# A decode kernel with gradients: products that stream 8 or 16 columns in place of 64, larger score units, and another order for the w1 rows

## The chip, the cores and the metric

The kernel runs on one core of one Trainium2 chip. The metric is the time of one execution on the device, in microseconds. The kernel before was timed three times: 2059.57, 2062.02 and 2064.87 us, median 2062.02. One execution was also recorded by the hardware profiler.

TensorE (PE in the profile) multiplies: it loads a 128 x 128 block as weights (PEld) and then streams the columns of the other operand past it. VectorE (DVE) and ScalarE (ACT) copy, reduce and evaluate functions. GpSimd (POOL) copies here and issues the output transfers. SyncE (SP) issues the input transfers. A transfer is a DMA.

## The reference

Two layers, attention and a squared-ReLU MLP, are run twice over with the same weights on one token of width 1024, and then everything is differentiated.

```
x = A_x
x = x + attention(layernorm(x), K, V, wq, wo)     # L1
x = x + mlp(layernorm(x), w1, b1, w2, b2)         # L2
x = x + attention(layernorm(x), K, V, wq, wo)     # L3, the same K and V
x = x + mlp(layernorm(x), w1, b1, w2, b2)         # L4
outputs: x, and the gradients of x, K, V, wq, wo, w1, b1, w2, b2 for a given grad_out
```

The attention has 32 query heads of width 128 in 4 groups of 8; each group shares one K and one V of 65,536 keys. K and V are 64 MiB each, in bfloat16. A score is q.k / sqrt(128), then a softmax over all 65,536 keys, then the sum of V with these weights. Both attention layers read the same K and V, so the gradients of K and V are sums over the two.

## The kernel before, in words

**Chunks, items, groups.** A chunk is 128 keys: one 128 x 128 block of K and one of V. A group has 512 chunks (`C`), an item is 8 chunks, so a group has 64 items (`IPG`). K and V come in slabs of 32 chunks (1 MB) into slots of SBUF. A `Ring` hands out the least recently used slot; SP issues the loads in program order and stands still until the slot of the next load is free. The slots are `area[0]` to `area[13]`; 6 to 13 are halves of four pairs.

**Four passes over K and V.** The forward of L1, the forward of L3, pass 3 (the backward of L3, `attn_bwd3`) and pass 4 (the backward of L1, which also forms the gradients of K and V for both layers, `attn_bwd4`). `pipeline` (line 455) writes the order out: at step i each stage of a pass works on item i minus its lag, and then the background tasks due at this step (`bg`, filled by `at`) are emitted. Every engine follows that order.

**Forward (`attn_fwd`, line 517).** `kT` transposes the 8 blocks of an item on TensorE, and ACT or DVE copies them out of PSUM (`evac` picks the less loaded of the two, lines 153 and 156). `kS`, two steps later, multiplies each transposed block with the group's queries. The 8 queries of a group are 8 columns, but `L["qpad"]` holds them 8 times over, 64 columns, and all 64 are streamed (line 557). The product of chunk c is written to the columns of slot c and of the seven slots behind it; the next chunk overwrites those, and only the first 8 columns of each remain. For that a bank of 64 slots holds a unit of 56 chunks (`UB`). After a unit ACT copies its scores to SBUF and DVE takes their maximum (lines 562 and 563). After the last unit of a group `stats` takes the exponentials, 8 on ACT (line 586). `v8`, 12 steps after the group's last scores, multiplies V with the weights: 8 heads by 8 neighbouring chunks, 64 columns, of which 8 are used (line 600).

**Pass 3.** V is transposed (line 741) and multiplied with the gradient of the output (`vS`, line 761): 64 columns, where `dOpad` has zeros in all but the first 8, so the rest adds nothing. A first product per unit writes a bias to the whole bank (line 757). DVE multiplies with the weights (line 767), and `k8` multiplies K with the result (line 783), again 64 columns with 8 used.

**Pass 4** does this for both layers at once: 16 columns used of 64 in `vS` (line 855, `DOB`), units of 24 chunks (`UB4`), 8 of 64 in `k8` (line 893). Per unit DVE forms X (lines 864 and 865, with copies by GpSimd in 866 and 867), TensorE transposes X (line 872), and two products of 512 columns for every four chunks form the gradients of K and V (line 899), which ACT and DVE copy to a staging slot and GpSimd sends out (906, 907). X has three buffers (`XS`), its transposes three (`XT`). The weight gradients (`outer2`, line 949) run as background tasks.

**The w1 rows of L4 (`fetch_w1`, line 997).** L4 needs w1 as eight blocks of rows of 917 KB. They are fetched at the end of the forward of L3, in background steps counted from `ik`, the step after the last score product. Scores of a group are kept in a pair of slots: the third group's in slots 12 and 13, the last group's in 10 and 11, where the exponentials read them.

Of the kernel before, what the change touches and what calls it, by code (L numbers as in the profile page):

```python
# [8 lines left out]
BF = mybir.dt.bfloat16  # L9
# [9 lines left out]
def kernel(  # L19
# [42 lines left out]
    SLOTS = 512 // R  # L62
    UB = SLOTS - 8
# [3 lines left out]
    SL4 = 512 // R2  # L67
    UB4 = SL4 - 8
# [409 lines left out]
    def set_q(L, pq, at_, gs):  # L478
        for i, g in enumerate(gs):
            nc.vector.tensor_copy(out=L["qT"][:, g * R:(g + 1) * R], in_=pq[:, (at_ + i) * R:(at_ + i + 1) * R])  # L480
            nc.vector.tensor_copy(out=L["qpad"][:, g, :, :], in_=L["qT"][:, g * R:(g + 1) * R].unsqueeze(1).to_broadcast([P, 8, R]))
# [26 lines left out]
    def new_layer(x, lname):  # L508
# [4 lines left out]
        L["qpad"] = vec.tile([P, G, 8, R], BF, name=lname + "_qpad")  # L513
# [3 lines left out]
    def attn_fwd(L, order, eT, s_areas, more=None, keep=(), have=()):  # L517
# [26 lines left out]
        def kS(idx):  # L544
            g, c8 = kit[idx]
            if c8 == 0:
                state["S"] = s_areas[order.index(g) % 2].bitcast(F32).rearrange("p (r c) -> p r c", c=C)
                state["pm"] = tmp.tile([P, R, (C + UB - 1) // UB], F32, name="pm_all")
            S_sb, pm_all = state["S"], state["pm"]
            kt = state.pop(("kt", idx))  # L550
            for i in range(8):
                c = c8 + i
                slot = c % UB
                if slot == 0:
                    state["ps_s"] = ps_sc([P, SLOTS, R])
                ps_s = state["ps_s"]
                nc.tensor.matmul(ps_s[:, slot:slot + 8, :].rearrange("p a b -> p (a b)"), lhsT=kt[:, i, :],  # L557
                                 rhs=L["qpad"][:, g, :, :].rearrange("p a b -> p (a b)"), start=True, stop=True)
                if slot == UB - 1 or c == C - 1:
# [165 lines left out]
    def attn_bwd3(L, og, order, eT, dqT, bg):  # L725
# [6 lines left out]
        dOpad = vec.tile([P, G, 8, R], BF, name=lname + "_dOpad")  # L732
        nc.vector.memset(dOpad[:], 0.0)
# [12 lines left out]
        def vS(idx):  # L746
            g, c8 = kit[idx]
            if c8 == 0:
                nc.vector.tensor_copy(out=dOpad[:, g, 0, :], in_=og.dOT[:, g * R:(g + 1) * R])
                nc.vector.tensor_copy(out=ndt[:, :, :], in_=og.nd2[:, g * R:(g + 1) * R].unsqueeze(1).to_broadcast([64, SLOTS, R]))  # L750
            vt = state.pop(("vt", idx))
            for i in range(8):
                c = c8 + i
                slot = c % UB
                if slot == 0:
                    state["ps_dp"] = ps_sc([P, SLOTS, R])
# [3 lines left out]
                last = (slot == UB - 1 or c == C - 1)  # L760
                nc.tensor.matmul(ps_dp[:, slot:slot + 8, :].rearrange("p a b -> p (a b)"), lhsT=vt[:, i, :],  # L761
                                 rhs=dOpad[:, g, :, :].rearrange("p a b -> p (a b)"), start=False, stop=last)
                if last:
                    un = slot + 1
                    c0 = c - slot
                    dsT = dst.next().rearrange("p (s r) -> p s r", r=R)
                    nc.vector.tensor_tensor(out=dsT[:, 0:un + 8, :], in0=ps_dp[:, 0:un + 8, :],
                                            in1=eT[g][:, :, c0:c0 + un + 8].rearrange("p h c -> p c h"), op=ALU.mult)
                    add_load(dve=0.07 + (un + 8) * R * 0.0019)
                    state[(g, c0 // UB)] = dsT  # L770

        def k8(idx):
# [4 lines left out]
            if c8 == 0:  # L777
                state["ps_dq"] = ps_acc([P, 8, R])
            ps_dq = state["ps_dq"]
            for i in range(8):  # L780
                c = c8 + i
                sl = c - u * UB
                nc.tensor.matmul(ps_dq[:, :, :].rearrange("p a b -> p (a b)"), lhsT=kb8[:, i, :],
                                 rhs=dsT[:, sl:sl + 8, :].rearrange("p a b -> p (a b)"), start=(c == 0), stop=(c == C - 1))
            if c8 + 8 == C:
                nc.vector.scalar_tensor_tensor(out=dqT[:, g * R:(g + 1) * R], in0=ps_dq[:, 0, :], scalar=SCALE,
# [4 lines left out]
    def attn_bwd4(La, Lb, oga, ogb, order, eTa, eTb, dqT, bg, group_done, streams):  # L791
# [4 lines left out]
        XT = Turn([blocks(small, i) for i in range(3, 6)])  # L796
        XW = (UB4 + 1) * R4
        XS = Turn([part(small[:, 6144:], i, XW) for i in range(2)] + [part(area[5], 0, XW)])
        GGS = Turn([part(area[5][:, XW:], i, 512) for i in range(2)])
        NSL = UB4 + 4  # L800
        ndt4 = small[0:64, 6144 + 2 * XW:6144 + 2 * XW + NSL * R2].rearrange("p (s r) -> p s r", r=R2)
        ST = Turn([pair[6], pair[8], pair[10]])
        DOB = vec.tile([P, G, 4, R2], BF, name="DOB")
# [391 lines left out]
```

## Time and profile before

| | |
|---|---|
| profiled execution | 2060.59 us |
| its span, first to last instruction | 2058.8 us |
| median of the three timed runs | 2062.02 us |
| mean granted TensorE clock | 0.898 |
| TensorE busy | 1636.8 us (80%) |
| VectorE, ScalarE, GpSimd busy | 1139.3, 1037.8, 200.4 us |
| moved by DMA | 809.62 MB, mean 393 GB/s |

The granted clock is the share of the TensorE clock that a throttle let through: 1.0 or 0.5 at any moment, and the mean over a window or slice in the tables. "DMA share" is the mean busy share of the core's 16 DMA engines. In a list of instructions "x24" counts them; "<-" behind an idle time names what ended it.

### The profile page before, as it was taken

The page shows a single profiled execution, that of the slowest core. Times are in us where ns is not written, and L with a number is a line of the kernel's source. Part 1 is how long each engine was busy: PE and PEld are TensorE (multiplying, and loading weights), DVE is VectorE, ACT ScalarE, POOL GpSimd, SP SyncE. Part 2 cuts the span into 40 slices and gives each one's busy share as a digit, 9 for nine tenths or more (in the row PEclk, how much of TensorE's full clock was granted, in tenths as well). Part 3 has the DMA queues.
Part 4 walks back from the last instruction along what each step waited for, and adds up shares of the span by engine and source line. Part 5 has one row for each costly group of instructions (what it writes and reads, how often), then busy time and mean ns, then how long its engine had stood idle before and what let it go on. Part 6 is the DMA issues. An engine that isn't in the chain of part 4 may idle for free.

```text
span 2058.8 us, 66212 instructions
## 1 busy us (share of the span) xinstructions
PE 1636.8 (80%) x29852; PEld 1332.2 (65%) x29852; DVE 1139.3 (55%) x1887; ACT 1037.8 (50%) x1325; POOL 200.4 (10%) x386
## 2 busy tenths in 40 slices
PE   7888886588898847788888765779888978988876
PEld 7878776578787737677777664456555545655544
DVE  4544431255444303744444557668777767768856
ACT  4543432125433302444444537768666756767855
POOL 0000000000000000000000001213222222222221
PEclk9999997579999956899999987989999999998988
DMA  9999999999999998999999997899999999998996
GB/s 381 416 417 414 412 417 407 392 358 416 414 415 414 383 392 312 345 417 414 414 417 387 401 387 309 342 347 422 401 423 417 413 424 384 424 422 339 424 423 275
DMA packets 140079, 809.62 MB, mean 393 GB/s; under 512 B 13844, under 2 KB 13844, under 8 KB 58644
## 3 DMA queue, kind: packets, MB, share of 16 engines
q1 hardware_dynamic: 112884, 639.70, 76.7%
q0 software_dynamic: 26912, 165.69, 19.7%
q8 instruction: 233, 3.82, 0.7%
q14 instruction: 50, 0.41, 0.0%
HBM read 639.64 MB, written 165.69 MB: 391 GB/s over the span
## 4 chain that ended last, share of the span: by engine, by line
DMA 41%; PE 31%; ACT 12%; DVE 10%; issue 5%; SPq 0%; POOL 0%; ACTq 0%; DVEq 0%; POOLq 0%
DMA out_dram<-pair 11%; DMA slot<-in_A_k_cache_dram 7%; DMA slot<-in_A_v_cache_dram 7%; DMA pair<-in_A_v_cache_dram 5%; PE ps_tr L539 5%; PE ps_sc L557 4%; ACT small L153 4%; DMA pair<-in_A_k_cache_dram 3%; DMA pair<-in_A_wo_dram 3%; PE ps_gg L899 3%; PE ps_acc L600 2%; PE ps_tr L836 2%; ACT pair L153 2%; PE ps_tr L741 2%; DVE pair L156 2%
## 5 line engine op out<-in xcount | busy, mean ns | idle before, releaser
L156 DVE COPY small<-ps_tr 128x1024 bf16<-128x1024 bf16 (+1 forms) x650 | 438.8, 686 | 387.5 <-PE ps_tr L539 207.5
L153 ACT COPY small<-ps_tr 128x1024 bf16<-128x1024 bf16 (+1 forms) x414 | 394.5, 967 | 431.3 <-PE ps_tr L539 248.8
L153 ACT CAST pair<-ps_gg 128x1024 bf16<-128x1024 f32 x289 | 289.9, 1015 | 144.5 <-PE ps_gg L899 100.5
L156 DVE CAST pair<-ps_gg 128x1024 bf16<-128x1024 f32 x223 | 272.3, 1221 | 105.2 <-PE ps_gg L899 79.1
L899 PE MATMUL ps_gg<-slot,small 64*128 64x512 bf16 x1024 | 202.8, 400 | 69.8 <-ACT pair L153 30.1
L557 PE MATMUL ps_sc<-L_qpad,small 128*128 128x64 bf16 x3712 | 178.4, 196 | 26.3 <-ACT small L153 14.0
L539 PE MATMUL ps_tr<-ident_b,slot 128*128 128x128 bf16 x2304 | 163.1, 224 | 15.5 <-DMA slot<-in_A_k_cache_dram 11.5
L557 PEld LDWEIGHTS <-small 128*128 128x128 bf16 x3712 | 141.8, 99 | 45.1 <-ACT small L153 25.2
L600 PE MATMUL ps_acc<-eT,slot 128*128 128x64 bf16 x2720 | 131.1, 210 | 44.9 <-DMA slot<-in_A_v_cache_dram 42.3
L539 PEld LDWEIGHTS <-slot 128*128 128x128 bf16 x2304 | 137.2, 100 | 17.5 <-DMA slot<-in_A_k_cache_dram 14.1
L600 PEld LDWEIGHTS <-slot 128*128 128x128 bf16 x2720 | 114.9, 107 | 49.4 <-DMA slot<-in_A_v_cache_dram 46.6
L899 PEld LDWEIGHTS <-small 64*128 64x128 bf16 x1024 | 58.4, 94 | 112.5 <-issue 82.1
L836 PE MATMUL ps_tr<-ident_b,slot 128*128 128x128 bf16 x1440 | 128.3, 229 | 0.4 <-DVE small L156 0.2
L539 PE MATMUL ps_tr<-ident_b,pair 128*128 128x128 bf16 x1600 | 114.3, 224 | 14.4 <-DMA pair<-in_A_k_cache_dram 13.7
L836 PEld LDWEIGHTS <-slot 128*128 128x128 bf16 x1440 | 90.8, 102 | 50.6 <-issue 46.5
L761 PE MATMUL ps_sc<-B_dOpad,small 128*128 128x64 bf16 x2048 | 101.0, 196 | 25.4 <-ACT small L153 17.6
L855 PE MATMUL ps_sc<-DOB,small 128*128 128x64 bf16 x2048 | 118.1, 198 | 0.0
L855 PEld LDWEIGHTS <-small 128*128 128x128 bf16 x2048 | 92.4, 101 | 35.9 <-issue 27.3
L539 PEld LDWEIGHTS <-pair 128*128 128x128 bf16 x1600 | 95.4, 100 | 17.4 <-DMA pair<-in_A_k_cache_dram 15.4
L761 PEld LDWEIGHTS <-small 128*128 128x128 bf16 x2048 | 78.6, 100 | 42.9 <-ACT small L153 27.2
L949 PE MATMUL ps_gg<-pair 128*128 128x512 bf16 x240 | 80.0, 412 | 27.9 <-ACT pair L153 16.1
L382 ACT ACTIVATE slot<-slot 128x1024 bf16<-128x1024 bf16 (+1 forms) x75 | 84.1, 1123 | 19.1 <-DVE slot L381 18.4
(275 smaller groups left out, 2437.6 us busy)
## 6 DMA issues: line engine op xcount, KB each, us to landing
slot<-in_A_v_cache_dram SPq DMA_DIRECT2D x164, 1024.0 KB, 17.7
slot<-in_A_k_cache_dram SPq DMA_DIRECT2D x159, 1024.0 KB, 11.8
out_dram<-pair POOLq DMA_DIRECT2D x128, 1024.0 KB, 17.8
pair<-in_A_k_cache_dram SPq DMA_DIRECT2D x82, 1024.0 KB, 19.9
pair<-in_A_v_cache_dram SPq DMA_DIRECT2D x80, 1024.0 KB, 20.0
out_dram<-eT POOLq DMA_DIRECT2D x41, 512.0 KB, 18.8
slot<-in_A_wq_dram SPq DMA_DIRECT2D x25, 768.0 KB, 11.1
slot<-in_A_wo_dram SPq DMA_DIRECT2D x16, 1024.0 KB, 12.8
```

The costliest lines, as they stand in the source:

```text
L153: nc.scalar.copy(out=out, in_=in_)
L156: nc.vector.tensor_copy(out=out, in_=in_)
L382: nc.scalar.activation(out=view, in_=view, func=ACTF.Copy, accum_out=ycol)
L539: nc.tensor.transpose(pt[:, i, :], kb8[:, i, :], ident_b[:, :])
L557: nc.tensor.matmul(ps_s[:, slot:slot + 8, :].rearrange("p a b -> p (a b)"), lhsT=kt[:, i, :], rhs=L["qpad"][:, g, :, :].rearrange("p a b - ...
L600: nc.tensor.matmul(ps_o[:, :, :].rearrange("p a b -> p (a b)"), lhsT=vb8[:, i, :], rhs=eT[g][:, :, c:c + 8], start=(c == 0), stop=(c == C ...
L741: nc.tensor.transpose(pt[:, i, :], vb8[:, i, :], ident_b[:, :])
L761: nc.tensor.matmul(ps_dp[:, slot:slot + 8, :].rearrange("p a b -> p (a b)"), lhsT=vt[:, i, :], rhs=dOpad[:, g, :, :].rearrange("p a b -> p ...
L836: nc.tensor.transpose(pt[:, i, :], vb8[:, i, :], ident_b[:, :])
L855: nc.tensor.matmul(ps_dp[:, slot:slot + 4, :].rearrange("p a b -> p (a b)"), lhsT=vt[:, i, :], rhs=DOB[:, g, :, :].rearrange("p a b -> p ( ...
L899: nc.tensor.matmul(pg[:, t2 * 512:(t2 + 1) * 512], lhsT=xt[64 * t2:64 * t2 + 64, blk0 + half, :], rhs=GG[64 * t2:64 * t2 + 64, :, :, :].re ...
L949: nc.tensor.matmul(pg[:, q0:q0 + qq], lhsT=av[:, kb + kk, :], rhs=b_rows[:, n0 + m0 + q0:n0 + m0 + q0 + qq], start=True, stop=True)
```

## The change

The products of `kS`, `vS` and `k8` stream only the columns that are used: 8, and 16 in pass 4's `vS`. The padded operands (`qpad`, `dOpad`, the wide `DOB`) become plain ones (`qb`, `dOb`, `DOB`). The value product of the forward (`v8`) keeps its 64 columns. As no slots behind a unit are needed any more, a unit fills its bank: 64 chunks in place of 56 in the forward and pass 3, and 32 in place of 24 in pass 4, so a group has 8 units (10 before) and 16 (22 before). The lag of `k8` follows from the unit: one step more in pass 3 and pass 4. In pass 4 X and its transposes have two buffers in place of three, all in `small`. The rows of w1 go to slots 12, 13, 10, 11, 9, 8, 7, 6 at steps 1, 3, 16, 20, 24, 28, 33, 38 behind `ik`; before, to 10, 11, 12, 13, 9, 8, 7, 6 at 1, 3, 5, 7, 12, 18, 24, 30. Slot 5 leaves the ring at step 44 in place of 36.

```diff
-    SLOTS = 512 // R
-    UB = SLOTS - 8
+    UB = 512 // R
...
-    SL4 = 512 // R2
-    UB4 = SL4 - 8
+    UB4 = 512 // R2
...
-            nc.vector.tensor_copy(out=L["qpad"][:, g, :, :], in_=L["qT"][:, g * R:(g + 1) * R].unsqueeze(1).to_broadcast([P, 8, R]))
+            nc.vector.tensor_copy(out=L["qb"][:, g * R:(g + 1) * R], in_=L["qT"][:, g * R:(g + 1) * R])
...
-                nc.tensor.matmul(ps_s[:, slot:slot + 8, :].rearrange("p a b -> p (a b)"), lhsT=kt[:, i, :],
-                                 rhs=L["qpad"][:, g, :, :].rearrange("p a b -> p (a b)"), start=True, stop=True)
-                if slot == UB - 1 or c == C - 1:
+                nc.tensor.matmul(ps_s[:, slot, :], lhsT=kt[:, i, :], rhs=L["qb"][:, g * R:(g + 1) * R], start=True, stop=True)
+                if slot == UB - 1:
...
-                nc.tensor.matmul(ps_dp[:, slot:slot + 8, :].rearrange("p a b -> p (a b)"), lhsT=vt[:, i, :],
-                                 rhs=dOpad[:, g, :, :].rearrange("p a b -> p (a b)"), start=False, stop=last)
+                nc.tensor.matmul(ps_dp[:, slot, :], lhsT=vt[:, i, :], rhs=dOb[:, g * R:(g + 1) * R], start=False, stop=last)
...
-                nc.tensor.matmul(ps_dq[:, :, :].rearrange("p a b -> p (a b)"), lhsT=kb8[:, i, :],
-                                 rhs=dsT[:, sl:sl + 8, :].rearrange("p a b -> p (a b)"), start=(c == 0), stop=(c == C - 1))
+                nc.tensor.matmul(ps_dq[:, :], lhsT=kb8[:, i, :], rhs=dsT[:, c - u * UB, :], start=(c == 0), stop=(c == C - 1))
...
-        XT = Turn([blocks(small, i) for i in range(3, 6)])
-        XW = (UB4 + 1) * R4
-        XS = Turn([part(small[:, 6144:], i, XW) for i in range(2)] + [part(area[5], 0, XW)])
+        XT = Turn([blocks(small, i) for i in (3, 4)])
+        XS = Turn([part(small, i, 1024) for i in (5, 6)])
...
-                nc.tensor.matmul(ps_dp[:, slot:slot + 4, :].rearrange("p a b -> p (a b)"), lhsT=vt[:, i, :],
-                                 rhs=DOB[:, g, :, :].rearrange("p a b -> p (a b)"), start=False, stop=last)
+                nc.tensor.matmul(ps_dp[:, slot, :], lhsT=vt[:, i, :], rhs=DOB[:, g, :], start=False, stop=last)
...
-                nc.tensor.matmul(ps_dq[:, :, :].rearrange("p a b -> p (a b)"), lhsT=kb8[:, i, :],
-                                 rhs=X[:, sl:sl + 2, :].rearrange("p a b -> p (a b)"), start=(c == 0), stop=(c == C - 1))
+                nc.tensor.matmul(ps_dq[:, :], lhsT=kb8[:, i, :], rhs=X[:, c - u * UB4, 0:R], start=(c == 0), stop=(c == C - 1))
...
-        for k, i in enumerate((10, 11, 12, 13)):
-            at(bg, ik + 1 + 2 * k, lambda i=i: one(area[i]))
         at(bg, ik + 2, lambda: ring.remove(*area[6:10]))
-        for k, i in enumerate((9, 8, 7, 6)):
-            at(bg, ik + 12 + 6 * k, lambda i=i: one(area[i]))
-        at(bg, ik + 36, lambda: ring.remove(area[5]))
+        for k, i in ((1, 12), (3, 13), (16, 10), (20, 11), (24, 9), (28, 8), (33, 7), (38, 6)):
+            at(bg, ik + k, lambda i=i: one(area[i]))
+        at(bg, ik + 44, lambda: ring.remove(area[5]))
...
-    LAG4 = 6
+    LAG4 = 7
```

## The prediction

> **What bounds the kernel now.** I read the page first, then a table of stages, then the clock in its own steps.
>
> ```profile
> PEclk9999997579999956899999987989999999998988
> DMA  9999999999999998999999997899999999998996
> ...
> HBM read 639.64 MB, written 165.69 MB: 391 GB/s over the span
> ...
> DMA 41%; PE 31%; ACT 12%; DVE 10%; issue 5%; SPq 0%; POOL 0%; ACTq 0%; DVEq 0%; POOLq 0%
> ```
>
> The DMA engines are full in nearly every slice, and the granted TensorE clock is high in nearly every slice. The windows of the stages say it sharper (after each engine's busy time: granted clock, DMA share, GB/s):
>
> ```profile
> 27.00:330.00 303.00, 253.02 (x5732) 236.75 (x5730) 130.58 (x229) 129.79 (x192) 0.00 (x0) 0.96 1.01 413
> 460.00:710.00 250.00, 215.24 (x4931) 203.07 (x4927) 113.21 (x196) 106.93 (x156) 0.00 (x0) 0.97 1.01 415
> 850.00:1215.00 365.00, 302.00 (x6393) 269.88 (x6390) 184.74 (x297) 158.53 (x204) 0.00 (x0) 0.95 1.00 405
> 1280.00:1390.00 110.00, 81.41 (x1080) 53.98 (x1079) 76.01 (x116) 80.37 (x107) 22.26 (x42) 0.89 0.86 327
> 1390.00:1850.00 460.00, 399.39 (x5151) 258.03 (x5152) 346.55 (x484) 314.81 (x337) 124.47 (x237) 0.96 1.01 414
> 1850.00:2050.00 200.00, 160.55 (x1904) 101.69 (x1903) 152.29 (x212) 141.41 (x177) 45.71 (x86) 0.88 0.92 379
> ```
>
> Rows one and two are the forward passes, three is pass 3, four to six are pass 4. Memory traffic sets the pace except in row four and parts of row six. So fewer streamed columns buy nothing directly; what they can do is move the clock. The clock changes only at edges 3.41 us apart. Cut at those edges, a stretch with 64-column products alone (counts behind the first two busy times: matmuls and their weight loads):
>
> ```profile
> 351.42:354.83 3.41, 2.65 (x47) 2.49 (x48) 0.00 (x0) 0.00 (x0) 0.00 (x0) 0.50 1.01 420
> 354.83:358.25 3.42, 2.82 (x54) 2.66 (x51) 0.00 (x0) 0.00 (x0) 0.00 (x0) 0.50 1.02 414
> 358.25:361.66 3.41, 1.54 (x40) 1.28 (x38) 0.00 (x0) 0.00 (x0) 0.00 (x0) 1.00 1.02 423
> 361.66:365.07 3.41, 2.74 (x52) 2.58 (x51) 0.00 (x0) 0.00 (x0) 0.00 (x0) 0.50 1.01 401
> 365.07:368.49 3.42, 1.86 (x49) 1.59 (x46) 0.00 (x0) 0.00 (x0) 0.00 (x0) 1.00 0.94 367
> ```
>
> A step with 51 to 54 products is followed by a full-clock step, one with 47 or fewer by a half-clock step. So a step must stream about 49 x 64, some 3,100 columns, or the next one runs at half speed. That is my reading of these rows; one later step with 53 was followed by half, so the edge is soft.
>
> **Which columns the clock sees after the change.** A chunk is 128 keys: 64 KB of K and V, 158 ns at 415 GB/s, 21.6 chunks in a step. Columns per chunk, before and after: forward 128 (transpose) + 64 (score) + 64 (value product, untouched) = 256, then 200; pass 3 128+64+64 = 256, then 144; pass 4 128+64+32+64 and two 512-column products per four chunks that run side by side (two in 0.39 us, as long as one; counted once, 128) = 416, then 312, plus 60 of the weight gradients (240 products of 512 over 2,048 chunks). Pass 4 takes (2,050-1,280)/2,048 = 376 ns a chunk, 9.1 chunks a step. So a step streams in the forward 4,320 columns (5,530 before), in pass 3 3,110 at best and 2,760 at its mean of 365/2,048 = 178 ns (4,900 to 5,530 before), in pass 4 3,380 (4,320 before). The forward stays clear of 3,100, pass 3 falls onto or under it, pass 4 comes close.
>
> **Prices.** At full clock a transpose takes 56 ns (24 in 1.34 us), a 64-column product 29 (24 loads in 0.76 us), a 1-column one 25 (64 in 1.58 us). At half clock: 107 (24 in 2.56 us), 53 (54 in 2.82 us), and
>
> ```profile
> 1225.79 6.12 PE ps_bg L1074 x224
> ```
>
> 27 ns for one column. No row has 8 or 16 columns; they lie between the 1-column and the 64-column rows, 25 to 29 ns and 27 to 53. 128 and 64 columns at half clock are in proportion (107, 53), which gives 7 ns for 8, so the 27 ns is a floor; I take 25 and 27. If the load were not hidden, 27+7 = 34.
>
> **Part 1, w1 rows.** SP stands in line with a row meant for slot 10, which the last group's exponentials still read:
>
> ```profile
> 693.68 2.82 SPq L250 DMA_DIRECT2D pair<-in_A_v_cache_dram  x2
> 698.69 0.33 SPq L250 DMA_DIRECT2D slot<-in_A_v_cache_dram  x1
> 701.19 23.88 SPq L1000 DMA_DIRECT2D pair<-in_B_w_dram  x4
> ```
>
> Queued behind it are V slabs. The DMA share in the four 5 us windows from 710 is 0.77, 0.51, 0.54, 0.94: 6.2 us idle. Afterwards rows go first to slots 12 and 13, long free, and SP passes on to three V slabs (2 x 0.92 + 3 x 1.05 = 5.0 MB, 12 us) before it meets slot 10. That spans 711 to 723 of a wait that ends at 724. The value stage that follows is fed by DMA to 794, so the gain stays. I take -5.5; bounds -6.2 and 0 (the V slabs' own slots free too late). A loss is excluded: the last row's issue moves 8 steps and still lies 38 steps before that stage's end.
>
> **Part 2, score units of 64.** Units fall from 10 to 8 a group, but the group's last one grows from 64 elements (ACT 0.22, DVE 0.22 us) to 512 (0.53 and 0.62 for 448, so 0.60 and 0.70): exponentials start 0.86 us later. Three of four groups hide it behind the 12-step lag of the value product; the last groups of both passes don't. Half-clock steps in the forward cost TensorE 107+27+53 = 187 ns a chunk against 158 supplied, 0.6 us a step, and ten slots of 1 MB hide that (without them, some 23 such steps, +14). I take +1; bounds 0 and +14.
>
> **Part 3, pass 3.** TensorE needs 56+25+25+3 (the broadcast product) = 109 ns a chunk at full clock, 107+27+27+7 = 168 at half; supply is 158 to 178. At half clock and never idle a step streams 3,413/168 x 144 = 2,930 columns: mostly it stays at half, and the order of transposes and products within a step lifts some over the edge. The cover is thin: in the last group, with the w2 transposes (224 x 107 = 24 us), half-clock TensorE needs 512 x 168 + 24 = 110 us, about the 114 that the DMA needs, and the ring has five slots. Bounds: 0 (full-clock steps catch up), and +32 (34 ns each, so 182 ns a chunk: 2,048 x 182 + 24 = 397 against 365). I take +7, near the lower end, where the 1-column row puts it. The lag one step longer (K loads behind V) adds at most one step of 1.3 us and is in it.
>
> **Part 4, pass 4.** In the order transpose, product with V, transpose of X, broadcast, product with K, wide pair, TensorE needs 56+29+15+8+29+54 = 191 ns a chunk before and 56+25+14+7+25+54 = 181 after at full clock, 364 and 308 at half (107+53+28+16+53+107; 107+27+27+13+27+107), with the weight gradients 50 more: 358, under the 376 supplied. From 1,390 to 1,850 the DMA hides it; if staging slots come later for it, +3. Where the DMA isn't full (1,280 to 1,390, 1,860 to 1,880, 2,020 to 2,050: 160 us, 55 steps of eight chunks) the clock lies on the path. A clock of 0.89 is 22% half-clock steps: 8 x (0.78 x 191 + 0.22 x 364) = 1.83 us a step; with 55% after, 8 x (0.45 x 181 + 0.55 x 308) = 2.01. 55 x 0.18 = +10 if TensorE were the whole path there; the chain gives it about a third: +4. Units fall from 88 to 64 with DVE products of 256 elements for 200 (0.49 us; at 1.8 ns an element more 0.60): 88 x 0.98 - 64 x 1.20 = 9 us of DVE, a fifth of it in those stretches: -2. Two X buffers in place of three wait for nothing new: a unit's last reader runs three steps before the next writer. Sum +5; bounds -10 and +20.
>
> The Trainium skill speaks against this reading. "TensorE: Matmul & The Clock Gate", Part 4: transposes don't count as busy for the clock. By that rule pass 3 would show the gate 16 columns a chunk and stay at half throughout, my second rival. The trace disagrees: the first two of these steps hold 28 transposes each and otherwise single columns, and the step after each has the full clock.
>
> ```profile
> 1238.89:1242.30 3.41, 2.15 (x28) 1.59 (x28) 1.00 1.03 425
> 1242.30:1245.71 3.41, 2.15 (x28) 1.60 (x28) 1.00 1.01 420
> 1245.71:1249.13 3.42, 0.38 (x4) 0.23 (x4) 1.00 1.00 406
> ```
>
> **The sum.** -5.5 + 1 + 7 + 5 = +7.5 on the profiled execution of 2060.6 (span 2058.8, 1.8 around it): 2068.1. The median of the runs, 2062.0, is 1.4 higher: 2069.5, said as 2070.
>
> **Rivals.** Clock stuck: pass 3 stays at half and TensorE sets its pace. For it: 2,930 columns are under the edge. Against: it must need more than the supply. With 34 ns products +32 there, +10 in pass 4 (the whole path, above), -5.5: 2062 + 36.5 = 2098, or 2088 with pass 3 alone. Cover holds: slots and DMA hide every half-clock step and only part 1 is left: 2062 - 5.5 = 2056.5; for it, full DMA in nine tenths of the stages' time. Faster: half-clock steps themselves get cheaper (364 to 308). If their share stays at 25% where the DMA isn't full, a step there takes 8 x (0.75 x 181 + 0.25 x 308) = 1.70 for 1.83, 55 steps give -7, with part 1 2049; it decides below a share of 38%. Against: pass 4 falls to 3,380 columns a step. The w1 order does nothing, if SP then waits as long at slot 10 later, and the rest cancels: 2062.
>
> **How the numbers follow.** About 0.3% (6.2 us) is what a measurement of this kernel can tell from no change. Forecast (2063 to 2080) 0.42, of it 0.32 slower and 0.10 within; clock stuck 0.18, slower; cover holds 0.24, 0.14 faster and 0.10 within; faster 0.14; nothing 0.02, within. Together faster 0.28, within 0.22, slower 0.50. The range 2050 to 2096 leaves out the far ends of the stuck clock and of the faster case, some 0.17. The forecast's own range is 2063 to 2080.
>
> **What would show it.** Granted clock in pass 3 from 0.95 to about 0.6 to 0.75, with DMA share still 0.97 or more there (more idle DMA: stuck); forward clock 0.88 or more; pass 4 about 0.8. No DMA gap at 710 to 725. L783 at 27 ns in half-clock steps. A clock that stays at 0.9 in pass 3 makes my reading of the gate wrong; more than 385 us for pass 3 makes the 27 ns or the cover wrong.

## The result and the profile after

The changed kernel takes 2092.59 us (median of four runs, 2090.20 to 2096.58), the kernel before 2061.08 (2059.57 to 2064.87): a ratio of 1.0152, 95% interval 1.0129 to 1.0175. It is slower by some 31 us, where 8 were forecast; 2092.6 lies in the range of 2050 to 2096, near its far end, and outside the forecast's own 2063 to 2080. The profiled execution took 2090.20 us with a span of 2088.4, the mean granted clock is 0.809 (0.898 before).

From the page of the changed kernel, the clock and the DMA by slices, the traffic, and the chain by engine:

```profile
PEclk9999996569998855777767766876898889988896
DMA  9999999999999997999996998899999999999996
...
HBM read 639.64 MB, written 165.69 MB: 386 GB/s over the span
...
DMA 37%; PE 36%; DVE 12%; ACT 11%; issue 4%; POOL 0%; SPq 0%; DVEq 0%; ACTq 0%; POOLq 0%
```

The bytes are the same and move 1% slower on average. TensorE's share of the chain rose from 31% to 36%, DMA's fell from 41% to 37%. From the 17th slice on, at 835 us, the clock is lower than before in most slices. The same windows as before, of the changed kernel (behind the busy times: granted clock, DMA share, GB/s):

```profile
27.00:330.00 303.00, 253.10 (x5741) 235.25 (x5739) 128.67 (x221) 130.01 (x185) 0.00 (x0) 0.94 1.01 415
460.00:710.00 250.00, 217.58 (x4932) 204.27 (x4930) 110.37 (x191) 106.40 (x148) 0.00 (x0) 0.94 1.02 417
850.00:1215.00 365.00, 307.09 (x5909) 285.88 (x5907) 166.43 (x266) 147.96 (x188) 0.00 (x0) 0.74 0.95 377
1280.00:1390.00 110.00, 87.23 (x1134) 58.31 (x1135) 78.20 (x128) 74.75 (x94) 20.99 (x34) 0.74 0.81 308
1390.00:1850.00 460.00, 393.35 (x5085) 249.85 (x5082) 333.82 (x451) 306.76 (x329) 116.06 (x201) 0.87 1.00 407
1850.00:2050.00 200.00, 159.94 (x1984) 99.74 (x1985) 152.72 (x192) 143.56 (x173) 45.49 (x80) 0.83 0.98 403
```

Row three stands out: the clock of pass 3 fell from 0.95 to 0.74, and its traffic from 405 to 377 GB/s. The loss can be placed by SP's own list. SP issues the seventh slab of pass 3 at 827.7 us (833.6 before), so the changed kernel comes there 6 us early. The seventh slab of pass 4 is issued at 1273.4 (1251.3 before), 22 us late. Pass 3 lost 28 us. Inside it the lead of the loads shrinks slowly: 5 us at the 32nd load behind that one, 1.5 behind at the 64th, 6 to 8 behind at 1060. Up to 1060 the traffic is still that of the kernel before (409 GB/s from 850 to 1060 in both). Most of the loss in traffic shows at 1060 to 1130, 275 GB/s against 395. Windows of the changed kernel there, the second one a part of the first:

```profile
1060.00:1130.00 70.00, 62.57 (x1234) 58.94 (x1231) 25.49 (x37) 25.47 (x26) 0.00 (x0) 0.75 0.74 275
1105.00:1120.00 15.00, 13.63 (x290) 12.98 (x288) 4.97 (x7) 5.88 (x6) 0.00 (x0) 0.78 0.03 11
```

For 15 us almost nothing is loaded, while TensorE is busy for 13.6 of them. SP's list of the changed kernel has the reason (start, duration, line, transfer):

```profile
1099.75 0.64 SPq L248 DMA_DIRECT2D slot<-in_A_k_cache_dram  x1
1119.62 0.33 SPq L248 DMA_DIRECT2D slot<-in_A_v_cache_dram  x1
```

SP stands from 1100.4 to 1119.6 in front of a slot that still holds an earlier slab; in pass 3 only TensorE's transposes and products read the slabs. At this place of the program the ring shrinks from 13 slots to 5. The waits of SP from 850 to 1240 us that TensorE ended, by line (total us, times, longest; L737 is the transpose, L776 the product with K):

```profile
SPq L248 <- PE ps_tr L737: 136.3, 50, 5.4
SPq L248 <- PE ps_acc L776: 64.6, 32, 19.1
```

That is 201 us behind TensorE, and 58 behind the loads of slabs; in the kernel before it was 79 and 161. The loads of pass 3 used to wait for the DMA and now wait for TensorE.

**Why TensorE is late.** Cut at the clock's edges, six steps of the changed kernel in a row, all instructions (matmuls and weight loads counted behind the first two busy times):

```profile
1060.28:1063.69 3.41, 3.41 (x81) 3.41 (x80) 0.69 (x1) 2.02 (x2) 0.00 (x0) 0.50 1.03 413
1063.69:1067.10 3.41, 3.41 (x46) 3.41 (x43) 1.32 (x2) 1.01 (x1) 0.00 (x0) 0.50 1.00 360
1067.10:1070.52 3.42, 2.22 (x63) 1.83 (x62) 1.80 (x3) 0.00 (x0) 0.00 (x0) 1.00 0.96 347
1070.52:1073.93 3.41, 3.41 (x40) 3.41 (x41) 0.69 (x1) 1.75 (x2) 0.00 (x0) 0.50 0.94 368
1073.93:1077.34 3.41, 3.41 (x95) 3.30 (x93) 1.14 (x2) 1.50 (x3) 0.00 (x0) 1.00 0.87 312
1077.34:1080.76 3.42, 2.38 (x65) 1.94 (x62) 1.88 (x3) 0.76 (x1) 0.00 (x0) 1.00 0.91 299
```

The same steps, the transposes alone (line 737 of the changed kernel; PE, PEld, clock, DMA share, GB/s):

```profile
1060.28:1063.69 3.41, 1.93 (x17) 1.43 (x16) 0.50 1.03 413
1063.69:1067.10 3.41, 3.34 (x31) 3.12 (x32) 0.50 1.00 360
1067.10:1070.52 3.42, 0.37 (x6) 0.20 (x5) 1.00 0.96 347
1070.52:1073.93 3.41, 3.36 (x32) 3.09 (x32) 0.50 0.94 368
1073.93:1077.34 3.41, 1.89 (x31) 1.55 (x29) 1.00 0.87 312
1077.34:1080.76 3.42, 0.42 (x8) 0.25 (x5) 1.00 0.91 299
```

A step with 31 or 32 transposes (some 4,000 columns) is followed by full clock; a step with 6 transposes and otherwise products of 8 columns is followed by half. The first of these steps shows that being busy isn't enough: it is busy for all its 3.41 us with 81 products, but 17 transposes make at most some 2,700 columns, and the next step is at half clock. So the steps mostly alternate, and in the unlucky way: full clock falls to the products, which gain nothing from it (25 ns against 27), and half clock falls to the transposes, which cost twice as much. In the 57 steps from 862 to 1057 us, 31 are half-clock steps. Counted by their start, 626 of the 1,032 transposes, 61%, lie in them, but 37% of the products with V and 23% of the products with K. In the same 57 steps the edge can be bracketed, with the bias product as 512 columns: each step that streamed fewer than 3,104 columns was followed by half clock, each one with more than 3,456 by full clock, and between them both occur.

The second half of the answer is in the full-clock steps with few transposes: TensorE is idle in them for some 30% of the time. At 1069 us, lines of the changed kernel's timeline (the unit's DVE product, then the bias product that opens the next unit):

```profile
1069.04 1.04 DVE L761 TENSOR_TENSOR small<-ps_sc,eT 128x512 bf16<-128x512 f32 x1 [0.85 <-PE ps_sc L757]
...
1070.13 0.37 PE L753 MATMUL ps_sc<-small,sel 64*128 64x512 bf16 x1 [0.73 <-DVE small L761]
```

What TensorE waits for from 860 to 1060 (total us, times, longest):

```profile
PE ps_sc L753 <- DVE small L761: 15.7, 17, 2.2
PE ps_mv L644 <- DVE dlt_prod L642: 7.7, 2, 3.9
PE ps_sc L757 <- ACT small L151: 5.5, 18, 0.5
PE ps_sc L757 <- DVE small L154: 4.8, 15, 0.4
```

Together 33.7 us in 200, and no wait on a DMA among them. Counted by their start, the 57 steps hold 1,032 transposes, 1,056 products with V and 1,049 with K, on average 1,046 chunks: 194.6 us / 1,046 = 186 ns a chunk. The prices give a transpose of 0.6 x 107 + 0.4 x 56 = 87 ns, two products at about 26 and the bias product at about 6: 145. The waits, 33.7 / 200 of the time, add 31: 176. Ten ns are left over. A part of them lies in how the profile ends a burst: eight products of 25 ns stand in it with 0.35 us (at 1118.83), 0.15 more than their price, and only then does a wait begin; with 52 waits that is an estimated 7 ns a chunk. The kernel before took 166 ns a chunk in its 57 steps there, with the DMA full. TensorE is the bound of pass 3, and slots that were filled ahead hid it from the traffic until 1060.

### The profile page after: what moved, and what is told of

It is laid out like the page before. It is cut to its first block, busy times and chain, and to the rows that moved or that the text cites. A ratio compares the mean times of both kernels' runs of the same rounds, so it can differ in the third digit from the quotient of the medians.

```text
span 2088.4 us, 65902 instructions
## 1 busy us (share of the span) xinstructions
PE 1673.7 (80%) x29820; PEld 1362.0 (65%) x29820; DVE 1125.5 (54%) x1814; ACT 1028.0 (49%) x1284; POOL 190.1 (9%) x338
## 4 chain that ended last, share of the span: by engine, by line
DMA 37%; PE 36%; DVE 12%; ACT 11%; issue 4%; POOL 0%; SPq 0%; DVEq 0%; ACTq 0%; POOLq 0%
DMA out_dram<-pair 13%; PE ps_tr L737 7%; DMA slot<-in_A_k_cache_dram 6%; PE ps_tr L537 5%; DMA slot<-in_A_v_cache_dram 4%; DMA pair<-in_A_k_cache_dram 4%; ACT small L151 4%; DVE small L154 3%; DMA pair<-in_A_wo_dram 3%; PE ps_gg L883 3%; PE ps_sc L555 3%; PE ps_tr L825 3%; PE ps_acc L597 2%; DVE pair L154 2%; PE ps_sc L757 2%
## 5 line engine op out<-in xcount | busy, mean ns | idle before, releaser
L154 DVE COPY small<-ps_tr 128x1024 bf16<-128x1024 bf16 x654 | 440.0, 687 | 380.7 <-PE ps_tr L537 172.3
L151 ACT COPY small<-ps_tr 128x1024 bf16<-128x1024 bf16 x386 | 387.6, 1015 | 432.4 <-PE ps_tr L537 227.4
L154 DVE CAST pair<-ps_gg 128x1024 bf16<-128x1024 f32 x215 | 261.9, 1221 | 101.0 <-PE ps_gg L883 76.0
L883 PE MATMUL ps_gg<-slot,small 64*128 64x512 bf16 x1024 | 220.9, 437 | 78.7 <-DVE pair L154 39.4
L555 PE MATMUL ps_sc<-L_qb,small 128*128 128x8 bf16 x3712 | 160.0, 167 | 36.4 <-DVE small L154 18.8
L537 PE MATMUL ps_tr<-ident_b,slot 128*128 128x128 bf16 x2304 | 167.0, 228 | 14.0 <-DMA slot<-in_A_k_cache_dram 10.5
L555 PEld LDWEIGHTS <-small 128*128 128x128 bf16 x3712 | 131.7, 97 | 60.0 <-DVE small L154 25.2
L537 PEld LDWEIGHTS <-slot 128*128 128x128 bf16 x2304 | 141.3, 102 | 17.4 <-DMA slot<-in_A_k_cache_dram 13.0
L825 PE MATMUL ps_tr<-ident_b,slot 128*128 128x128 bf16 x1440 | 148.2, 239 | 1.8 <-DVE small L154 1.2
L597 PEld LDWEIGHTS <-slot 128*128 128x128 bf16 x2720 | 116.4, 108 | 40.9 <-DMA slot<-in_A_v_cache_dram 39.2
L825 PEld LDWEIGHTS <-slot 128*128 128x128 bf16 x1440 | 99.6, 106 | 53.0 <-issue 47.0
L757 PE MATMUL ps_sc<-B_dOb,small 128*128 128x8 bf16 x2048 | 89.9, 169 | 24.1 <-ACT small L151 12.9
L737 PE MATMUL ps_tr<-ident_b,slot 128*128 128x128 bf16 x1088 | 106.5, 269 | 3.4 <-ACT small L151 2.2
L844 PEld LDWEIGHTS <-small 128*128 128x128 bf16 x2048 | 81.5, 99 | 38.4 <-issue 34.7
L737 PEld LDWEIGHTS <-slot 128*128 128x128 bf16 x1088 | 90.1, 124 | 22.5 <-issue 22.4
L560 DVE TENSOR_REDUCE pm_all<-pair 128x8 f32<-128x512 f32 x64 | 43.9, 686 | 110.4 <-ACT pair L559 110.4
```

Source lines behind the costliest of these rows:

```text
L151: nc.scalar.copy(out=out, in_=in_)
L154: nc.vector.tensor_copy(out=out, in_=in_)
L537: nc.tensor.transpose(pt[:, i, :], kb8[:, i, :], ident_b[:, :])
L555: nc.tensor.matmul(ps_s[:, slot, :], lhsT=kt[:, i, :], rhs=L["qb"][:, g * R:(g + 1) * R], start=True, stop=True)
L560: nc.vector.tensor_reduce(out=pm_all[:, :, c0 // UB], in_=S_sb[:, :, c0:c0 + un], axis=AX.X, op=ALU.max)
L597: nc.tensor.matmul(ps_o[:, :, :].rearrange("p a b -> p (a b)"), lhsT=vb8[:, i, :], rhs=eT[g][:, :, c:c + 8], start=(c == 0), stop=(c == C ...
```

## The experiments

Each kernel was run beside the kernel before on the same chip; ratios are to that one. There were two chips; the kernel before took 2059.55 to 2059.79 us on them (medians), so kernels are also compared with each other. The base is the kernel before for five of them and the changed kernel for the other seven. The fences show the main lines of each edit.

### The four parts one by one

**The w1 rows alone.** The kernel before, with the new order of the rows:

```diff
-        for k, i in enumerate((10, 11, 12, 13)):
-            at(bg, ik + 1 + 2 * k, lambda i=i: one(area[i]))
...
+        for k, i in ((1, 12), (3, 13), (16, 10), (20, 11), (24, 9), (28, 8), (33, 7), (38, 6)):
+            at(bg, ik + k, lambda i=i: one(area[i]))
...
```

> The kernel before with the new order of the w1 rows and nothing else. Theory: the 6.2 us in which DMA stood idle while SP waited for slot 10 are gone, so 5 to 6 us faster than before: about 2055.5 (2054.5 to 2057), DMA share at 0.98 or more in 710 to 725. Rival: SP waits as long at slot 10 a little later: 2060 or more.

Measured: 2055.42 us (ten runs) against 2059.55, ratio 0.998 (0.9971 to 0.999): 4.1 us gained. SP's list of this kernel shows that it now passes on to three V slabs before it stops:

```profile
698.98 2.80 SPq L1000 DMA_DIRECT2D pair<-in_B_w_dram  x2
703.96 5.30 SPq L250 DMA_DIRECT2D slot<-in_A_v_cache_dram  x3
721.26 0.33 SPq L1000 DMA_DIRECT2D pair<-in_B_w_dram  x1
```

The four windows of 5 us from 710 have DMA shares of 1.02, 0.99, 0.83 and 1.01, some 5.3 us less idle than before; the third still falls short of the expected 0.98. This part did what the forecast said.

**The forward alone** (units of 64 chunks, 8 columns in `kS`; passes 3 and 4 and the w1 rows as before):

```diff
-                nc.tensor.matmul(ps_s[:, slot:slot + 8, :].rearrange("p a b -> p (a b)"), lhsT=kt[:, i, :],
-                                 rhs=L["qpad"][:, g, :, :].rearrange("p a b -> p (a b)"), start=True, stop=True)
+                nc.tensor.matmul(ps_s[:, slot, :], lhsT=kt[:, i, :], rhs=L["qb"][:, g * R:(g + 1) * R], start=True, stop=True)
```

> The kernel before with the changed forward alone (8 columns in the scores, units of 64). Predicted +1, since ten slots hide a half-clock step: 2059 to 2063, DMA share 1.01 in both passes, clock 0.94. Rival: half-clock steps or the later exponentials reach the end, 2065 or more.

Measured: 2061.65 us (ten runs) against 2059.73, ratio 1.0007 (0.9997 to 1.0017). No difference that can be told from none.

**Pass 3 alone** (units of 64, 8 columns in `vS` and `k8` of `attn_bwd3`):

```diff
-                nc.tensor.matmul(ps_dp[:, slot:slot + 8, :].rearrange("p a b -> p (a b)"), lhsT=vt[:, i, :],
-                                 rhs=dOpad[:, g, :, :].rearrange("p a b -> p (a b)"), start=False, stop=last)
+                nc.tensor.matmul(ps_dp[:, slot, :], lhsT=vt[:, i, :], rhs=dOb[:, g * R:(g + 1) * R], start=False, stop=last)
...
-                nc.tensor.matmul(ps_dq[:, :, :].rearrange("p a b -> p (a b)"), lhsT=kb8[:, i, :],
-                                 rhs=dsT[:, sl:sl + 8, :].rearrange("p a b -> p (a b)"), start=(c == 0), stop=(c == C - 1))
+                nc.tensor.matmul(ps_dq[:, :], lhsT=kb8[:, i, :], rhs=dsT[:, c - u * U64, :], start=(c == 0), stop=(c == C - 1))
```

> The kernel before with the changed pass 3 alone (8 columns in both products, units of 64, lag one step longer). Theory: the changed kernel reaches pass 3 6 us earlier and leaves it 21 us later than before, so pass 3 alone costs 25 to 28 us: about 2087 (2082 to 2091), granted clock in pass 3 about 0.74, a DMA gap of some 16 us near 1100. Rival (the loss belongs to pass 4 and to what one pass leaves to the next): under 2075.

Measured: 2090.90 us against 2059.55, ratio 1.0155 (1.0139 to 1.017): the whole loss of the change, in this one part. Its clock is 0.73 from 850 to 1215.

**Pass 4 alone** (units of 32, 16 columns in `vS`, 8 in `k8`, two X buffers, the longer lag):

```diff
-                nc.tensor.matmul(ps_dp[:, slot:slot + 4, :].rearrange("p a b -> p (a b)"), lhsT=vt[:, i, :],
-                                 rhs=DOB[:, g, :, :].rearrange("p a b -> p (a b)"), start=False, stop=last)
+                nc.tensor.matmul(ps_dp[:, slot, :], lhsT=vt[:, i, :], rhs=DOB[:, g, :], start=False, stop=last)
...
-                nc.tensor.matmul(ps_dq[:, :, :].rearrange("p a b -> p (a b)"), lhsT=kb8[:, i, :],
-                                 rhs=X[:, sl:sl + 2, :].rearrange("p a b -> p (a b)"), start=(c == 0), stop=(c == C - 1))
+                nc.tensor.matmul(ps_dq[:, :], lhsT=kb8[:, i, :], rhs=X[:, c - u * U32, 0:R], start=(c == 0), stop=(c == C - 1))
```

> The kernel before with the changed pass 4 alone (16 and 8 columns, units of 32, two X buffers, lag one step longer). The predicted sum put +5 on it: 2063 to 2067. The runs so far put more on it: the changed kernel with a wide product with K in pass 3 (2071.7) and the kernel before with the new w1 order (2055.4) reach pass 4 at the same moment, 1248 us, and differ by 16 behind it: 2071 to 2078. Clock from 1390 to 1850 0.87 for 0.96 in both cases.

Measured: 2063.92 us (ten runs, 2058.75 to 2072.72) against 2059.73, ratio 1.0024 (1.001 to 1.0037): 4.2 us lost. The expectation, taken from differences between earlier runs, was too high. The four medians add up to -4.1 + 1.9 + 31.3 + 4.2 = +33, against +31.5 for the whole change.

### Columns or units?

The kernel before, with 8 columns in pass 3, but units of 56 chunks and the old lag:

```diff
-                nc.tensor.matmul(ps_dp[:, slot:slot + 8, :].rearrange("p a b -> p (a b)"), lhsT=vt[:, i, :],
-                                 rhs=dOpad[:, g, :, :].rearrange("p a b -> p (a b)"), start=False, stop=last)
+                nc.tensor.matmul(ps_dp[:, slot, :], lhsT=vt[:, i, :], rhs=dOpad[:, g, 0, :], start=False, stop=last)
...
-                nc.tensor.matmul(ps_dq[:, :, :].rearrange("p a b -> p (a b)"), lhsT=kb8[:, i, :],
-                                 rhs=dsT[:, sl:sl + 8, :].rearrange("p a b -> p (a b)"), start=(c == 0), stop=(c == C - 1))
+                nc.tensor.matmul(ps_dq[:, 0, :], lhsT=kb8[:, i, :], rhs=dsT[:, sl, :], start=(c == 0), stop=(c == C - 1))
```

> The kernel before, its pass 3 with units of 56 and its lag, but both products stream 8 columns. Theory (the columns set the clock, and the clock the loss): as with the whole changed pass 3, about 2085 (2078 to 2091), clock in pass 3 0.70 to 0.78. Rival (larger units, whose last DVE product TensorE waits for, and the longer lag): within 4 us of before, 2058 to 2066.

Measured: 2090.17 us, ratio 1.0148 (1.0133 to 1.0163). As much as with units of 64. It is the columns. The clock is as low as in the changed kernel:

```profile
850.00:1060.00 210.00, 182.99 (x3681) 168.81 (x3680) 102.10 (x171) 80.49 (x102) 0.00 (x0) 0.75 1.00 406
```

### Give the columns back without giving back anything else

The changed kernel, with `k8` of pass 3 streaming the same 8 columns eight times over. Nothing new is computed; TensorE has more to do.

```diff
-                state["ps_dq"] = ps_acc([P, R])
+                state["ps_dq"] = ps_acc([P, 8, R])
...
-                nc.tensor.matmul(ps_dq[:, :], lhsT=kb8[:, i, :], rhs=dsT[:, c - u * UB, :], start=(c == 0), stop=(c == C - 1))
+                nc.tensor.matmul(ps_dq[:, :, :].rearrange("p a b -> p (a b)"), lhsT=kb8[:, i, :],
+                                 rhs=dsT[:, c - u * UB, :].unsqueeze(1).to_broadcast([P, 8, R]), start=(c == 0), stop=(c == C - 1))
```

> The changed kernel, but the product with K in pass 3 streams its 8 columns eight times over (64 columns, the same weights, the same units of 64, the same lag): more work for TensorE, 200 columns a chunk for 144. Theory: 21.6 x 200 = 4,320 columns a step are clear of 3,100, the clock in pass 3 is 0.9 or more, the loss in pass 3 is gone and the w1 gain stays: about 2068 (2063 to 2074). Rival (units, lag, or the work itself): no faster than the changed kernel, 2090 or more.

Measured: 2071.72 us, ratio 1.0054 (1.0037 to 1.0072), 21 us faster than the changed kernel. Windows of this kernel in pass 3:

```profile
850.00:1060.00 210.00, 170.75 (x3800) 154.05 (x3798) 100.41 (x170) 82.74 (x102) 0.00 (x0) 0.95 1.00 410
1060.00:1130.00 70.00, 56.96 (x1254) 51.16 (x1254) 33.26 (x50) 30.00 (x36) 0.00 (x0) 0.98 0.98 394
```

The clock is back at 0.95 and the gap in the loads is gone. Pass 4 is reached at 1248.2 us, the same as with the w1 rows alone, so all of pass 3's loss is undone. From its first transpose to its last, pass 3 takes 368 us here, 368 in the kernel before and 394 in the changed kernel. The waits are not smaller: from 860 to 1060 TensorE waits 38.4 us (33.7 in the changed kernel), led by the same one.

```profile
PE ps_sc L753 <- DVE small L761: 14.7, 18, 2.1
PE ps_sc L757 <- ACT small L151: 9.3, 31, 0.6
PE ps_mv L644 <- DVE dlt_prod L642: 7.6, 2, 3.8
PE ps_sc L757 <- DVE small L154: 4.5, 14, 0.4
PE ps_acc L776 <- issue: 2.3, 2, 1.4
```

What changed is the transposes: 6 of 57 steps are at half clock, and 147 of the 1,134 transposes, 13%, start in them. The account for a chunk is 0.13 x 107 + 0.87 x 56 = 63 for the transpose, 25 and 29 for the products, 5 for the bias, and 33 of waits: 155 ns. The steps show 170 (194.6 us for 1,147 chunks); with 67 waits an estimated 9 of the 15 left over are again the ends of bursts. 170 is about what the DMA supplies, as the kernel before had 166. Against the 186 of the changed kernel that is 16 ns on 2,048 chunks, 33 us, where the pass as a whole became 26 us shorter.

The rest, that this kernel stays about 10 us above what the parts alone would give (2059.6 - 4 + 2 + 4 = 2061.5), lies behind 1248 us, in pass 4, which the next kernel changes.

**The same in pass 4 as well.** On top of the last edit:

```diff
-                nc.tensor.matmul(ps_dq[:, :], lhsT=kb8[:, i, :], rhs=X[:, c - u * UB4, 0:R], start=(c == 0), stop=(c == C - 1))
+                nc.tensor.matmul(ps_dq[:, :, :].rearrange("p a b -> p (a b)"), lhsT=kb8[:, i, :],
+                                 rhs=X[:, c - u * UB4, 0:R].unsqueeze(1).to_broadcast([P, 8, R]), start=(c == 0), stop=(c == C - 1))
```

> The changed kernel with the product with K streaming its 8 columns eight times over in pass 3 and in pass 4 as well: 368 columns a chunk in pass 4 for 312, with the weight gradients 9.1 x 428 = 3,900 a step for 3,380; units of 32, two X buffers and the lag stay. If pass 4's loss is the clock too: clock there 0.91 or more and most of the 16 us gone, 2057 to 2064. If it is the units, the buffers or the lag: as with pass 3 alone widened, 2069 or more.

Measured: 2051.68 us (six runs), ratio 0.9958 (0.9945 to 0.9972). It beats both kernels: 41 us faster than the changed one, 8 faster than the one before; half of the 8 is what the w1 rows give alone, and where the other half comes from was not tested. It is also faster than the expected 2057 to 2064. Pass 4 from 1390 to 1850 in this kernel:

```profile
1390.00:1850.00 460.00, 388.48 (x5093) 252.38 (x5145) 340.32 (x449) 306.54 (x321) 117.31 (x204) 0.93 1.00 410
```

The clock there rose from 0.87 to 0.93. The edit in pass 4 brought 20 us, while narrowing pass 4 alone had cost only 4. Why the narrow pass 4 costs more beside the other parts was not settled. It varies from run to run (over 14 us in ten runs of pass 4 alone).

### Did the ring's shrinking make the loss, or only show it?

The changed kernel with five slots through all of pass 3:

```diff
-    ring.add(*area[6:14])
...
-    at(bg, i0 - 6, lambda: ring.remove(*area[6:14]))
```

> The changed kernel with five slots for K and V all through pass 3, in place of 13 that shrink to five in the third quarter of it. Theory (TensorE is late all along, the 13 slots only put the bill off until they shrink): the gap of some 16 us in the DMA near 1105 to 1120 is gone, DMA share under 1.0 from 870 on instead, and the end within 8 us of the changed kernel, 2085 to 2100. Rival (the sudden shrinking itself costs the time): 2070 to 2080.

Measured: 2101.93 us, ratio 1.0206 (1.0184 to 1.0228), 9 us more than the changed kernel and slightly above the expected span. Windows of this kernel:

```profile
850.00:1060.00 210.00, 172.31 (x3333) 160.91 (x3333) 92.22 (x147) 77.40 (x100) 0.00 (x0) 0.71 0.98 379
1105.00:1120.00 15.00, 13.91 (x279) 13.43 (x277) 4.73 (x7) 5.27 (x6) 0.00 (x0) 0.69 0.98 369
```

The gap at 1105 is gone and the traffic is lower all along (379 GB/s from 850 to 1060, 409 in the changed kernel). The first transpose of pass 3 comes at the same time, 835 us, though its seventh slab is issued 23 us later, as fewer slots are free; the last transpose comes 9.5 us later and the seventh slab of pass 4, at 1283.3, 10 us later. So the 13 slots only put the bill off: the loads ran ahead of TensorE until the ring shrank. The 9 us more are what the smaller ring costs.

### The wait for DVE

To lengthen that wait alone, the DVE product of a unit in pass 3 is done twice, the second time with the same result:

```diff
                     nc.vector.tensor_tensor(out=dsT[:, :, :], in0=ps_dp[:, :, :],
                                             in1=eT[g][:, :, c0:c0 + UB].rearrange("p h c -> p c h"), op=ALU.mult)
+                    nc.vector.tensor_tensor(out=dsT[:, :, :], in0=ps_dp[:, :, :],
+                                            in1=eT[g][:, :, c0:c0 + UB].rearrange("p h c -> p c h"), op=ALU.mult)
```

There are 32 units at 1.04 us each, 33 us. First in the changed kernel:

> The changed kernel with the DVE product behind each unit of pass 3 done twice (32 more of 1.05 us, 34 us of DVE). TensorE waits for this product before it starts the next unit. Theory: in pass 3 of the changed kernel TensorE with its waits is what is late, so a longer wait goes to the end nearly whole: +20 to +34, 2112 to 2127. Rival (TensorE needs 140 ns a chunk by its prices and has room): under 2100.

Measured: 2124.66 us, ratio 1.03 (1.028 to 1.0321), 32 us over the changed kernel. The wait lies on the path, to its full length. Then in the kernel with the wide K products in passes 3 and 4, where I held that TensorE had room for it:

> The same doubled DVE product in the kernel with both wide products with K (2051.7). Theory: with the clock up, TensorE has some 12 ns a chunk to spare against 158, the longer wait takes 16 more and is mostly hidden: 2052 to 2062. Rival: the wait costs the same in both, 2072 or more.

Measured: 2094.23 us, ratio 1.0163 (1.0148 to 1.0178), 42.5 us over that kernel. My theory fell and the rival held, with a wait that cost even more than in the changed kernel. Waits from 860 to 1200 and a window of this kernel:

```profile
PE ps_sc L753 <- DVE small L763: 45.9, 25, 3.1
```

```profile
950.00:1060.00 110.00, 83.23 (x1643) 76.17 (x1643) 52.36 (x79) 40.57 (x52) 0.00 (x0) 0.84 0.97 376
```

And the same of the kernel with the wide products and the single DVE product:

```profile
PE ps_sc L753 <- DVE small L761: 20.5, 27, 2.0
```

```profile
950.00:1060.00 110.00, 91.02 (x1978) 82.11 (x1975) 48.06 (x79) 44.72 (x53) 0.00 (x0) 0.91 1.02 417
```

The wait grew by 25 us between 860 and 1200, and the clock fell beside it, from 0.91 to 0.84: an idle TensorE streams no columns either. Even with the clock up, the 170 ns that a chunk took above are about what the DMA leaves, so there is no room. That the fallen clock accounts for the 10 us beyond 33 was not tested by itself.

### How many columns?

`k8` of pass 3 streams its columns four times (32), pass 4 as above eight times:

```diff
-                                 rhs=dsT[:, c - u * UB, :].unsqueeze(1).to_broadcast([P, 8, R]), start=(c == 0), stop=(c == C - 1))
+                                 rhs=dsT[:, c - u * UB, :].unsqueeze(1).to_broadcast([P, 4, R]), start=(c == 0), stop=(c == C - 1))
```

> The kernel with both wide products with K, but in pass 3 the 8 columns stream four times over in place of eight: 168 columns a chunk, 3,630 a step at the peak rate and 3,230 at pass 3's mean, both over 3,100. If the gate is an edge near 3,100: most of pass 3's 31 us stay away, 2053 to 2062, clock in pass 3 0.85 or more. If the loss goes in proportion to the columns missing: some 18 of the 31 come back, 2066 to 2073.

Measured: 2060.93 us (ten runs), ratio 0.9998 (0.9986 to 1.0011), 9 us over the kernel with 64. A window of this kernel:

```profile
950.00:1060.00 110.00, 88.80 (x1849) 80.76 (x1850) 46.91 (x82) 42.07 (x52) 0.00 (x0) 0.79 1.02 418
```

The time is the one expected for an edge (2053 to 2062), but the clock is not: 0.79, where 0.85 or more was expected. With 144 columns a chunk (the changed kernel) the clock in this window is 0.70, with 168 0.79, with 200 0.91. In time 168 columns cost 9 us against 200. What 144 cost against 200 was measured in one kernel only, with the narrow pass 4, as 21 us; pass 3 alone, from 256 to 144, cost 31. In proportion 168 would cost 12 to 18. So more than half of the loss is gone at 168, but how sharp the edge is these runs don't settle. Last, 128 columns in `k8` of pass 4, with pass 3 at 64:

```diff
-                                 rhs=X[:, c - u * UB4, 0:R].unsqueeze(1).to_broadcast([P, 8, R]), start=(c == 0), stop=(c == C - 1))
+                                 rhs=X[:, c - u * UB4, 0:R].unsqueeze(1).to_broadcast([P, 16, R]), start=(c == 0), stop=(c == C - 1))
```

> The kernel with both wide products with K, in pass 4 sixteen times over: 128 columns, with the weight gradients 492 a chunk, 4,470 a step for 3,900. Clock from 1390 to 1850 0.95 or more for 0.93. If what is left of pass 4's loss is the clock: 2046 to 2051. If TensorE's 27 ns more a chunk (55 us over the pass) come through instead: 2056 or more.

Measured: 2059.44 us (ten runs), ratio 0.9996 (0.9982 to 1.0009), 8 us over the kernel with 64. Its window:

```profile
1390.00:1850.00 460.00, 408.59 (x5091) 272.47 (x5141) 343.32 (x455) 310.90 (x327) 118.35 (x206) 0.97 1.01 413
```

The clock rose further, to 0.97, and TensorE was busy for 20 us more, and that came through, as the second half of the expectation had it: here more columns only cost.

## Why the prediction was right and wrong

**The number.** That 2092.6 lies between 2050 and 2096 is owed to the breadth of the range, which was drawn for the stuck clock and its products of 34 ns. The sum was 23 us short, nearly all of it in part 3.

**What bounds the kernel; the gate.** Right. The reading that a step of 3.41 us must stream some 3,100 columns or be followed by half clock carried the case: pass 3 showed 0.74, inside the 0.6 to 0.75 that was named, the forward 0.94 (0.88 or more), pass 4 0.74 to 0.87 (about 0.8). The rows behind the 3,100 count products that cross an edge in both steps; by their start the steps hold 47, 49, 36, 48 and 44, and those with 48 and 49 were followed by full clock, so the edge read there is nearer to 3,050. The kernel that streams 8 columns eight times over shows the cause, since it changes nothing but the columns of one product.

**Prices.** Right: back to back, the products of 8 columns follow each other at 25 ns at full and 27 at half clock in the changed kernel, the transposes at 56 and 107. The 34 ns of the upper bound were not seen.

**Part 1, -5.5.** Right: -4.1 for the end, 5.3 us of the gap closed.

**Part 2, +1.** Right within what can be told: +1.9, interval from -0.6 to +3.5.

**Part 3, +7.** This is the step that failed. Pass 3 alone measures +31, almost at the upper bound of +32, but not for that bound's reason. The need of TensorE, 109 ns at full and 168 at half clock, was made of prices alone and held against a supply of 158 to 178. Two things were missing. TensorE waits for DVE and ACT, 31 ns a chunk. It already waited 25.6 us from 860 to 1060 in the kernel before (waits on a DMA not counted; 21 ns a chunk), and the prediction gave that nothing. The two longest of these waits in the kernel before:

```profile
PE ps_sc L757 <- DVE small L767: 8.8, 9, 2.4
PE ps_mv L647 <- DVE dlt_prod L645: 6.6, 2, 3.6
```

And half-clock steps were taken as a fair sample of the work, with the order in a step even lifting some over the edge. In fact the order put 61% of the transposes into them and most of the products, which gain nothing from the clock, into the full ones. Full-clock steps caught up little, because TensorE was idle for 18 of their 89 us. With both, a chunk took 186 ns, more than the supply. The line "more than 385 us for pass 3 makes the 27 ns or the cover wrong" points the right way: 394 us from the first transpose to the last, with products at 27 ns, so it was the cover.

**The ring as cover.** The prediction saw five slots and a thin cover in the last group. It did not see that 13 slots before that were filled by loads ahead of TensorE, so that a DMA share of 1.00 at 850 to 1060 said nothing about who was behind; what SP waited for would have. "DMA share still 0.97 or more there" was wrong for the pass as a whole (0.95), at just the place where the ring shrinks.

**Part 4, +5.** Right for pass 4 alone: +4.2. It does not hold beside the other parts, where widening it again brought 20 us; that stays open.

**The rivals.** "Clock stuck" gave 2088 with pass 3 alone and 2098 with both, and 2092.6 lies between them. Its picture was nearer than the forecast's in one point, that TensorE sets the pace of pass 3. It was wrong in another, since the clock did not stay at half: it alternated. "Cover holds", "faster" and "nothing" are excluded by pass 3 alone.

**Transposes and the clock.** With 64 columns in `k8`, pass 3 streams 64 + 8 columns a chunk besides the transposes, some 1,450 in a step of 20 chunks, and has a clock of 0.95; and the steps at 1064 and 1071 us, almost all transposes, are each followed by full clock. The Trainium skill, "TensorE: Matmul & The Clock Gate", Part 4, says that transposes don't count as busy for the clock in the same way. This case's runs disagree, with one reserve: the profile lists the transposes as MATMUL and doesn't show in which mode they run.

## What to carry to other kernels

A product that streams fewer columns than it takes time to issue is not free to narrow: price the stage at both clocks, and add what TensorE waits for, before comparing with the supply of the DMA. A DMA share of 1.0 in front of a deep ring doesn't show who is behind; look at what the loads wait for, and at where the ring shrinks or runs full. Where the clock falls for want of columns, streaming the same columns several times can be the cheapest repair; in pass 4, 64 columns were better than 128, though the clock rose further with 128.

## What the runs showed of the hardware that was not expected

More work made the kernel faster: 56 more columns in each K product of pass 3 and pass 4 took it from 2092.6 to 2051.7 us. In pass 4, 128 columns cost 8 us against 64. The Trainium skill, "TensorE: Matmul & The Clock Gate", Part 1, "HAM oscillation — how this bites in real kernels", advises padding a thin M to 512 or more where the clock oscillates. The direction agrees; the sizes can't be compared, as M is there a dimension of the whole product, and here the columns of each product were widened.

A half-clock step is not a slower copy of a full one. Which work falls into it follows from what the step before streamed, so a regular order of transposes and narrow products can fall in with the gate's steps, with more of the wide work at half clock (61% of the transposes here) than of the narrow (23% of the products with K). And a wait on TensorE can cost more than its length (42.5 us for 33). The clock fell beside it; that this is the reason was not tested.
